# A list scheduler counts on more time between a transfer's wire time and its use, from the rolling pairs on

## Chip, core and metric

The kernel runs on one core of a Trainium2 chip. The metric is the device time of one execution in microseconds. Of the kernel before, three timed runs are shown, and one more execution that was recorded by the profiler.

## What is computed

Two blocks follow each other. The first is a retention attention without softmax, over 8 batches, 8 heads, 576 positions and a head dimension of 64, in float32. The second is a feed-forward block over the 4608 tokens, with a learned slope for negative values:

```python
scores = scale * np.matmul(q, k.transpose(0, 1, 3, 2))
Dmat = np.where(rel >= 0, gamma[:, None, None] ** rel[None, :, :], 0.0)
ret = scores * Dmat[None, :, :, :]
attn_out = np.matmul(ret, v)
# x: (B*S, H*D) = (4608, 512)
h = x @ w_in                                        # 512 x 2048
g = np.maximum(h, 0.0) + alpha * np.minimum(h, 0.0)
out = g @ w_out                                     # 2048 x 512
```

`rel` is the distance in positions between query and key, and each head has its own `gamma`. The two weight matrices arrive as 64-bit floats; the kernel reads them as pairs of 32-bit words and makes 32-bit floats of them on the chip.

## The kernel before

**Tiling.** The tokens are cut into 18 blocks of 256 (`kb`), the hidden dimension of 2048 into 8 units of 256 (`u`). A float32 operand of a large matmul is split into pieces of a shorter float format (a high part, a low part, and a difference), and three products of pieces replace one float32 product. Such a product is a matmul of 128 rows by 512 columns, L1187 and L1221 for the first layer and L1339 (in `second`) for the second layer.

**Stages.** A prologue computes the attention of the first two batches in wide pieces (`part_...`), converts the first 16 weight pieces, and runs eight cells in plain float32. Then come the *rolling pairs*: the other 24 head pairs of the attention, one after another, woven into the feed-forward work on the token blocks that are already finished, for the first half of the hidden units. The last stage runs the second half of the units for all blocks, two blocks side by side (`unit_two`), and needs no attention work any more.

**A head pair** is the function `joint`. Its keys and queries are loaded in eight pieces (`load_kq`, tiles `kx` and `qx`), its keys once more in another layout (`kn`), its values into `vn`. POOL scales `qx` (L832), DVE transposes both (L838), ACT scales `kn` (L843). TensorE then computes scores and sums over chunks of 64 positions (L919 and L922). DVE masks the scores into the tile `at` (L940); ACT and DVE accumulate the sums into `su` (L952 to L963). Two copies by DMA put the transposed queries beside the scores (`at<-qT`) and the sums beside the values (`vn<-su`). When they have landed, TensorE multiplies out the values (L860), and ACT copies these from the PSUM bank into the token block `x` (L879). `kx`, `qx`, `kn`, `kT`, `qT`, `at` and `su` have one buffer each, `vn` two.

**Weights.** Sixteen more pieces of the weights are converted between the pairs (`convert`): load into `op`, ACT (L729, L731), DVE (L739, L741, L750), POOL (L753), and a store from `wa` to the DRAM tile `wk`. They are read back after the pairs.

**What sets the order.** No order is written out. The kernel first records every operation as an `Op`, with its engine, a cost in microseconds, the operations that it depends on, and for a transfer a wire time `late` (bytes over a rate; 265 KB per us for most). `dues` then runs the list backward from the end and gives each operation a due time. `plan` runs it forward: on each engine, of the operations that can begin first, the one with the earliest due time is taken. Both ask `wait(d, op)` how long after `d` the operation `op` may begin: a constant if `d` is a transfer, nothing on the same engine, 0.2 us after TensorE, and 0.1 us otherwise. Twelve rounds of the two, and then 243 random shifts of the due times, keep the plan whose modelled total is the least. The operations are issued in that plan's order, on each engine's own queue; on the chip, semaphores make an instruction wait for what it needs, and planned times play no part.

Every transfer but one is issued on SP's queue, by the helper `dma` (L208). An instruction that waits there holds up all transfers behind it. TensorE's queue is in order too.

Of the kernel before, what the change touches and what calls it, by code (L numbers as in the profile page):

```python
# [21 lines left out]
def kernel(  # L22
# [24 lines left out]
    NKB = NTOK // TB  # L47
    NS = NU // 2
    NRING = 5

# [28 lines left out]
    def piece(x):  # L81
        return x.bitcast(PIECE)
# [35 lines left out]
    for i in range(NBIT - 1):  # L118
# [8 lines left out]
                            op=ALU.mult)  # L127
# [21 lines left out]

    ops = []

    class Op:
        def __init__(self, eng, cost, fn, deps, banks, late, lock, hold, size):
            self.eng, self.cost, self.fn, self.deps = eng, cost, fn, deps
            self.banks, self.late, self.lock, self.hold = banks, late, lock, hold
            self.size, self.n = size, len(ops)

    class Slot:  # L160
        def __init__(self, name, make, bank=False):
# [16 lines left out]
    def do(eng, cost, fn, r=(), w=(), late=0.0, lock=False, kind=None, hold=0.0, size=0):  # L178
        deps, gens = set(), []
        for keys, writes in ((r, False), (w, True)):  # L180
            for g, *sub in keys:
                wr, rd = g.keys.setdefault(tuple(sub), ([], []))
                deps.update(wr)
                if writes:
                    deps.update(rd)
                deps.update(g.before)
                if g not in gens:
                    gens.append(g)
        op = Op(eng, cost, fn, None, [g.slot for g in gens if g.slot and g.slot.bank], late, lock, hold,
                size)  # L190
        for g, *sub in w:
            g.keys[tuple(sub)] = ([op], [])
        for g, *sub in r:
            g.keys[tuple(sub)][1].append(op)
        for g in gens:
            assert not g.slot or g.slot.gen is g
            g.ops.append(op)
        op.deps = [d for d in deps if d is not op]
        op.gens, op.kind = gens, kind or eng
        ops.append(op)  # L200
        return op
# [22 lines left out]
    LAT = {"PE": 0.2}  # L224
# [1 line left out]
    users = []  # L226

    def wait(d, op):
        return 2.0 if d.late else 0.0 if d.eng == op.eng else LAT.get(d.eng, 0.1)

    def dues(after):
        users[:] = [[] for _ in ops]
# [11 lines left out]
        for _ in ops:  # L244
            pick = None
            for e, queue in ready.items():
                if queue:
                    t0 = min(max(free[e], can[op.n]) for op in queue)
                    op = max((op for op in queue if max(free[e], can[op.n]) <= t0 + 0.02),
                             key=lambda op: after[op.n])  # L250
                    t = max(free[e], can[op.n])
                    if pick is None or t < pick[0]:
                        pick = t, op
            t, op = pick
            ready[op.eng].remove(op)
            free[op.eng] = t + op.cost
            due[op.n] = -(t + op.cost)
            for d in op.deps:
                left[d.n] -= 1
                can[d.n] = max(can[d.n], t + op.cost + wait(d, op) + d.late)  # L260
                if not left[d.n]:
                    ready[d.eng].append(d)
# [88 lines left out]
    def slot(pool, tag, shape, dtype=FP32, bank=False):  # L351
        return Slot(tag, lambda: pool.tile(shape, dtype, tag=tag, name=f"{tag}_{next(serial)}"),
                    bank)
# [8 lines left out]
    def lx_all(which):  # L362
        if which not in lx_tiles:
            lx_tiles[which] = lpool.tile([P, 6 * NCC, TB], FP32, tag="lx", name=f"lx_{which}")
        return lx_tiles[which]

    def lx_slots(which):
        return [Slot(f"lx{n}", lambda n=n: lx_all(which)[:, 3 * NCC * n:3 * NCC * (n + 1)])
                for n in range(2)]
    lxs = lx_slots("w")  # L370
    xs = [slot(ring, f"x{n}", [P, NCC, TB]) for n in range(NRING)]
    os_ = [slot(ring, f"o{n}", [P, DM]) for n in range(2)]
# [180 lines left out]
    def chunk_home(x, j):  # L553
        kb, o = divmod(x // 3 * NJ + j, TB // C)
        if kb not in xb:
            xb[kb] = Gen(xs[kb % NRING])
        return xb[kb], o
# [240 lines left out]
    def load_kq(n):  # L798
        b, c = pairs[n]
        kx, qx = Gen(kxs), Gen(qxs)  # L800
        loaded[n] = [kx, qx, None, vnm[n % 2]]
        for g, src in ((qx, q), (kx, k)):
            for a in range(4):
                f0 = (a % 2) * 32
                dma(lambda g=g, a=a: g.get().rearrange("p (n r) -> p n r", r=32)[
                        32 * a:32 * a + 32],
                    lambda src=src, a=a, f0=f0: src[b, 2 * c + a // 2].rearrange(
                        "(n t) d -> t n d", t=32)[:, :, f0:f0 + 32], S * P, (), [(g, a)],
                    rate=RATE_128)

    def load_kn(n):
        b, c = pairs[n]
        kn = loaded[n][2] = Gen(kns)
        for h2 in range(2):
            dma(lambda h2=h2: kn.get()[half(1 - h2)],
                lambda h2=h2: k[b, 2 * c + h2].rearrange("(j t) d -> t j d", t=C), S * D * 4, (),
                [(kn, h2)], rate=RATE_256)
# [8 lines left out]
    def operands(n):  # L826
        c = pairs[n][1]
        kx, qx, kn, vn = loaded[n]

        def f():  # L830
            qh = qx.get().rearrange("p (j x r) -> p j x r", x=2, r=32)
            return nc.gpsimd.tensor_tensor(  # L832
                out=qh, in0=qh, in1=tabx[:, None, c, :, None].to_broadcast([P, NJ, 2, 32]),
                op=ALU.mult)
        do("POOL", 1.15, f, [(cst, "t")], [(qx, a) for a in range(4)], lock=True)
        kT, qT = turned[n] = Gen(kTs), Gen(qTs)
        for to, g in ((kT, kx), (qT, qx)):
            do("DVE", 0.77, lambda to=to, g=g: nc.vector.transpose(to.get(), g.get()),  # L838
               [(g, a) for a in range(4)], [(to, 0)])

        def f():
            t = kn.get().rearrange("p j d -> p (j d)")
            nc.scalar.activation(t, t, ACTF.Copy, scale=tabk[:, c:c + 1])  # L843
        do("ACT", 0.78, f, [(cst, "t")], [(kn, 0), (kn, 1)])
# [23 lines left out]
    def keep_x(n, pv, j1):  # L868
# [3 lines left out]
        while j < NJ:  # L872
            kb, o = divmod(b * NJ + j, w)
            if kb not in xb:
                xb[kb] = Gen(xs[kb % NRING])
            m, i = min(w - o, NJ - j), int(j >= j1)
# [114 lines left out]
    def fetch_x(vis):  # L991
        kb = vis["kb"]
        if kb in xb:
            x = xb.pop(kb)
            dma(lambda: x_kept[kb], lambda: x.get().rearrange("p c t -> p (c t)"), P * 4096,
                [(x, *s) for s in x.keys], [(xkm[kb], 0)], hold=HOLD_X)
        else:
            x = Gen(xs[taken[0] % 2])
            taken[0] += 1
            dma(lambda: x.get().rearrange("p c t -> p (c t)"), lambda: x_kept[kb], P * 4096,  # L1000
                [(xkm[kb], 0)], [(x, 0)])
        vis["from"] = x
# [137 lines left out]
    def row_x(side, l):  # L1140
        return (3 * side + (l if side else 2 - l)) * NCC

    def split_roll(vis):
        fetch_x(vis)
        x, side = vis["from"], vis["kb"] % 2
        g = vis["x"] = Gen(lxs[side])
        keys = [(x, *s) for s in x.keys]

        def view(l, n):
            r = row_x(side, l) + 2 * n  # L1150
            return lambda: lx_all("x")[:, r:r + 2]

        def raw(n):
            return x.get()[:, 2 * n:2 * n + 2]
        for n in range(2):
            h, l, d = (view(l, n) for l in range(3))
            do("ACT", 0.64, lambda n=n, h=h: nc.scalar.mul(piece(h()), raw(n), BELOW * 2.0 ** -12),
               keys, [(g, 0, n)])
            do("DVE", 0.70, lambda n=n, h=h, l=l: nc.vector.scalar_tensor_tensor(  # L1159
                out=piece(l()), in0=h(), scalar=-2.0 ** 12, in1=raw(n), op0=ALU.mult, op1=ALU.add),  # L1160
                keys + [(g, 0, n)], [(g, 1, n)], lock=True)
            do("POOL", 1.29, lambda h=h, l=l, d=d: nc.gpsimd.tensor_tensor(  # L1162
                out=piece(d()), in0=h(), in1=l(), op=ALU.subtract),
                [(g, 0, n), (g, 1, n)], [(g, 2, n)], lock=True)
# [222 lines left out]
    def joint_(x):  # L1387
        joint(x)
        done.add(x)
        if x + 1 < len(pairs):  # L1390
            load_kn(x + 1)
            operands(x + 1)
        if x + 2 < len(pairs):
            load_kq(x + 2)
# [219 lines left out]
        Gen(x).before = was_in  # L1614
    for _ in range(EARLY):
        joint_(next(todo))
    split_roll(visits[2])
    last = singles - 1
    t = 8
# [126 lines left out]
```

## Time and profile before

| what | us |
| --- | --- |
| median of three runs | 925.6 |
| lowest and highest run | 923.88 and 931.11 |
| the profiled execution's own time | 921.56 |
| its span | 919.6 |
| TensorE busy (share of the span) | 909.4 (99%) |
| weight loads | 737.3 (80%) |
| DVE, ACT, POOL busy | 547.3, 505.2, 519.5 |
| share of the 16 DMA engines' span, main queue | 52.4% |

The span is the time from the first instruction to the last; the execution's own time has 1.96 us around it. TensorE's busy time is made of modelled ends of pipelined matmuls, so that a short hole can be hidden in it; weight loads (PEld) lie beside the matmuls and have durations of their own. The profile also tells, for a transfer, the time from its issue to its landing, and for each wait which engine or transfer ended it. The first of the 24 scores blocks runs at about 90 us, the last values block at 439 us; from there to the end no pair is in the way.

### The profile page before, as it was taken

The numbers are of one execution on the slowest core, as the hardware profiler recorded it, in microseconds if no ns is written. First come the engines' busy times: TensorE is split into PE (matmuls) and PEld (weight loads), VectorE is DVE, ScalarE is ACT, GpSimd is POOL, SyncE is SP. The second block draws the span as 40 slices with busy tenths as digits, with TensorE's granted clock in tenths as the row PEclk, the third lists the DMA queues.
The fourth block names the chain that finished last, engine by engine and source line by source line (L and its number), as shares of the span: only waits on it lengthen the run. The fifth ranks groups of instructions, "written<-read, shape, count | busy, mean of one in ns | idle before, by whom it ended". The sixth has DMA issues, their size and how long they took to land. (4 is left out here: it accounts for less than half of the span.)

```text
span 919.6 us, 19101 instructions
## 1 busy us (share of the span) xinstructions
PE 909.4 (99%) x7289; PEld 737.3 (80%) x7289; DVE 547.3 (60%) x1003; ACT 505.2 (55%) x1010; POOL 519.5 (56%) x461
## 2 busy tenths in 40 slices
PE   8999999999999999999999999999999999999998
PEld 7776688888888887878888788888888888888886
DVE  6878767567676757576757776444444444444343
ACT  4575555646665655666746655536464636364441
POOL 4766746555565656666453247465656656574624
PEclk9999999999999999999999999999999999999999
DMA  9994787886898968885345331212221222211112
GB/s 214 262 230 80 181 194 173 192 185 143 178 186 204 207 137 215 168 183 159 127 143 190 116 116 56 92 57 81 81 79 43 95 95 68 84 54 47 47 46 68
DMA packets 235947, 121.32 MB, mean 132 GB/s; under 512 B 203456, under 2 KB 203728, under 8 KB 235856
## 3 DMA queue, kind: packets, MB, share of 16 engines
q1 hardware_dynamic: 235712, 119.98, 52.4%
q8 instruction: 57, 0.93, 0.5%
q14 instruction: 34, 0.28, 0.1%
q10 hardware_dynamic: 144, 0.13, 0.0%
HBM read 74.19 MB, written 32.51 MB: 116 GB/s over the span
## 5 line engine op out<-in xcount | busy, mean ns | idle before, releaser
L1339 PE MATMUL pso<-w,g 128*128 128x512 f32 x1392 | 339.2, 392 | 0.4
L1339 PEld LDWEIGHTS pso<-w,g 128*128 128x128 f32 x1392 | 259.0, 188 | 57.7 <-POOL g L1266 2.7
L1263 POOL TENSOR_TENSOR g<-ga_all,g 128x512 fp32r<-128x512 f32 x76 | 98.0, 1291 | 121.9 <-ACT g L1259 93.9
L1266 POOL TENSOR_TENSOR g<-g 128x512 fp32r<-128x512 f32 x114 | 147.3, 1293 | 16.6 <-DVE w L1065 4.4
L1187 PE MATMUL psh<-lx_x,w 128*128 128x512 f32 (+1 forms) x360 | 87.4, 381 | 0.0
L1187 PE MATMUL psa<-lx_x,w 128*128 128x512 f32 (+1 forms) x360 | 84.5, 375 | 0.0
L1187 PEld LDWEIGHTS psh<-lx_x,w 128*128 128x128 f32 x360 | 63.9, 188 | 13.9 <-issue 0.5
L1187 PEld LDWEIGHTS psa<-lx_x,w 128*128 128x128 f32 x360 | 64.7, 188 | 12.6 <-ACT kn L843 0.3
L1259 ACT ACTIVATE g<-ga_all 128x512 fp32r<-128x512 f32 x76 | 47.7, 631 | 41.6 <-PE pso L1339 21.8
L1162 POOL TENSOR_TENSOR lx_x<-lx_x 128x512 fp32r<-128x512 f32 x28 | 35.8, 1288 | 39.8 <-DVE lx_x L1159 36.9
L1263 POOL TENSOR_TENSOR g<-vn,g 128x512 fp32r<-128x512 f32 x25 | 32.4, 1294 | 41.9 <-ACT g L1259 37.4
L1255 POOL TENSOR_TENSOR g<-g 128x512 fp32r<-128x512 f32 x22 | 28.4, 1293 | 46.7 <-DVE g L1252 29.6
L940 DVE SCALAR_TENSOR_TENSOR at<-psa,pf,mask 64x512 f32<-64x512 f32 x48 | 36.0, 749 | 31.5 <-PE psa L919 27.1
L1339 PE MATMUL pso<-lx_x,g 128*128 128x512 f32 x216 | 53.3, 390 | 0.1
L1357 DVE TENSOR_TENSOR op<-pso,op 128x512 f32<-128x512 f32 x35 | 24.0, 685 | 41.4 <-PE pso L1339 41.3
L1261 ACT ACTIVATE g<-ga_all 128x512 fp32r<-128x512 f32 x76 | 47.2, 621 | 1.2 <-PE pso L1339 1.0
L1339 PEld LDWEIGHTS pso<-lx_x,g 128*128 128x128 f32 x216 | 40.4, 188 | 9.0 <-DVE o L1362 0.7
L753 POOL TENSOR_TENSOR wa<-wa,op 128x512 int32<-128x512 int32 x16 | 20.9, 1309 | 36.1 <-DVE wa L750 18.6
L860 PEld LDWEIGHTS psh<-at,vn 128*64 128x64 f32 x864 | 27.8, 137 | 10.0 <-issue 6.0
L1201 ACT COPY ga_all<-psh 128x512 f32<-128x512 f32 (+1 forms) x30 | 16.7, 557 | 33.0 <-PE psh L1187 26.1
L1221 PE MATMUL psh<-w,w 128*128 128x512 f32 x144 | 34.6, 389 | 0.0
L1221 PE MATMUL psa<-w,w 128*128 128x512 f32 x144 | 34.6, 389 | 0.0
(329 smaller groups left out, 1882.3 us busy)
## 6 DMA issues: line engine op xcount, KB each, us to landing
xk<-x SPq DMA_DIRECT2D x18, 512.0 KB, 4.0
ok<-o SPq DMA_DIRECT2D x36, 256.0 KB, 3.0
op<-ok SPq DMA_DIRECT2D x18, 512.0 KB, 3.9
out_dram<-o SPq DMA_DIRECT2D x35, 256.0 KB, 2.2
x<-xk SPq DMA_DIRECT2D x16, 512.0 KB, 4.8
qx<-in_q_dram SPq DMA_DIRECT2D x96, 72.0 KB, 3.2
kx<-in_k_dram SPq DMA_DIRECT2D x96, 72.0 KB, 3.4
kn<-in_k_dram SPq DMA_DIRECT2D x48, 144.0 KB, 3.6
```

Source lines behind the costliest of these rows:

```text
L860: nc.tensor.matmul(pv[i].get()[half(h2), (j - js[0]) * C:(j - js[0] + 1) * C], vns[n % 2][:, h2, j], mt.get()[:, h2, j], start=True, stop= ...
L940: nc.vector.scalar_tensor_tensor(out=mt.get()[half(1 - h2), h2, j], in0=fro[x], scalar=pf[x, 1, h:h + 1], in1=mask[x, None, :].to_broadcas ...
L1162: do("POOL", 1.29, lambda h=h, l=l, d=d: nc.gpsimd.tensor_tensor(out=piece(d()), in0=h(), in1=l(), op=ALU.subtract), [(g, 0, n), (g, 1, n) ...
L1187: nc.tensor.matmul(out_of(p), w[:, c0:c0 + P], xp(l, cc), start=(l != 1 and cc == 0), stop=(l > 0 and cc == NCC - 1))
L1221: nc.tensor.matmul(p.get(), w[:, c0:c0 + P], piece(words_of(g)[:, o:o + DM]), start=(l != 1 and cc == 0), stop=(l > 0 and cc == NCC - 1))
L1255: do("POOL", 1.29, lambda: nc.gpsimd.tensor_tensor(out=piece(to.get()[:, 2]), in0=to.get()[:, 0], in1=to.get()[:, 1], op=ALU.subtract), [( ...
L1259: do("ACT", 0.64, lambda: nc.scalar.mul(piece(to.get()[:, 2]), whole(), BELOW), both, [(to, 2)])
L1261: do("ACT", 0.64, lambda: nc.scalar.mul(piece(to.get()[:, 0]), whole(), BELOW * 2.0 ** -12), both, [(to, 0)])
L1263: do("POOL", 1.29, lambda: nc.gpsimd.tensor_tensor(out=piece(to.get()[:, 1]), in0=whole(), in1=to.get()[:, 2], op=ALU.subtract), both + [( ...
L1266: do("POOL", 1.29, lambda: nc.gpsimd.tensor_tensor(out=piece(to.get()[:, 2]), in0=to.get()[:, 0], in1=to.get()[:, 1], op=ALU.subtract), [( ...
L1339: nc.tensor.matmul(a[2 * m + b].get(), piece(g.get()[:, l, f, m * P:(m + 1) * P]), w_piece(u, 2 + f, l), start=(cell["first"] and f == 0 a ...
L1357: do("DVE", 0.69, lambda: nc.vector.tensor_tensor(out=t(), in0=p1.get(), in1=t(), op=ALU.subtract), [(p1, 0)], [tk])
```

## The change

From the moment at which the first rolling pair's work has been recorded, every new operation carries 3.5 instead of 2.0 as the time that the scheduler counts between the end of its wire time and its first use. Operations recorded earlier keep 2.0. The value is used in both directions, by `dues` and by `plan`. No operation, dependency, buffer or cost is altered otherwise.

```diff
     NRING = 5
+    LAND = 2.0, 3.5
...
-    ops = []
+    ops, land = [], [LAND[0]]
...
             self.banks, self.late, self.lock, self.hold = banks, late, lock, hold
-            self.size, self.n = size, len(ops)
+            self.size, self.n, self.land = size, len(ops), land[0]
...
     def wait(d, op):
-        return 2.0 if d.late else 0.0 if d.eng == op.eng else LAT.get(d.eng, 0.1)
+        return d.land if d.late else 0.0 if d.eng == op.eng else LAT.get(d.eng, 0.1)
...
     for _ in range(EARLY):
         joint_(next(todo))
+    land[0] = LAND[1]
     split_roll(visits[2])
```

The order in which each engine's instructions stand differs after the change almost from the first instruction, since due times are counted from the end.

## Prediction

> **What bounds the kernel now.** I read the page's first two parts for the busiest engine, then busy time in 20 us stretches, then the waits, then the time that transfers take to land.
>
> The first two parts of the page:
>
> ```profile
> span 919.6 us, 19101 instructions
> ...
> PE 909.4 (99%) x7289; PEld 737.3 (80%) x7289; DVE 547.3 (60%) x1003; ACT 505.2 (55%) x1010; POOL 519.5 (56%) x461
> ```
>
> TensorE is busy for 909.4 of 919.6 us, so 10.2 us are visibly idle. Where these lie is seen in stretches of 20 us (columns: span, busy us and count of PE, PEld, DVE, ACT, POOL, then the granted clock, DMA share and GB/s):
>
> ```profile
> 0.00:20.00 20.00, 15.94 (x345) 13.39 (x346) 11.58 (x51) 7.45 (x12) 8.91 (x22) 1.00 1.02 202
> ...
> 160.00:180.00 20.00, 19.90 (x185) 15.95 (x185) 13.07 (x24) 11.01 (x23) 8.71 (x7) 1.00 0.81 187
> ...
> 300.00:320.00 20.00, 20.00 (x274) 16.54 (x273) 15.23 (x29) 13.39 (x29) 12.80 (x11) 1.00 1.00 218
> ...
> 400.00:420.00 20.00, 19.51 (x177) 15.46 (x175) 14.40 (x28) 13.46 (x26) 11.27 (x9) 1.00 1.08 241
> ...
> 500.00:520.00 20.00, 19.86 (x87) 15.86 (x86) 14.55 (x23) 11.35 (x21) 6.32 (x5) 1.00 0.43 133
> ...
> 740.00:760.00 20.00, 20.00 (x90) 16.57 (x89) 8.35 (x12) 8.23 (x15) 9.09 (x9) 1.00 0.33 106
> ...
> 900.00:919.60 19.60, 15.55 (x69) 11.86 (x67) 7.99 (x13) 2.42 (x4) 6.92 (x6) 0.98 0.25 80
> ```
>
> The first stretch is idle for 4.06 us and the last for 4.05. Between 20 and 100 us it is 1.33 more (0.42 and 0.91), and from 100 to 900 us, where the change acts, 0.73 (0.10, 0.49 and 0.14). The modelled ends of matmuls can hide a hole, so I also compare weight loads with a full stretch: 740 to 760 has 16.57 us of them for 90 matmuls at 222 ns each. A stretch short of that by x has lost about x/16.57 of 20 us: 500 to 520 lost 0.86, the four stretches with 16.30 to 16.32 about 0.3 each. Among the rolling pairs, full stretches show 16.5; 160 to 180 lost 0.67 us and 400 to 420 lost 1.26, the four with 16.05 to 16.33 together 1.4. **All holes from 100 to 900 us come to 5.4 us**, 0.6% of the time.
>
> No wait of TensorE is charged to a transfer in the list of waits; the largest wait for one on any engine belongs to ScalarE, which is idle for it rather than late:
>
> ```profile
> ACT kn L843 <- DMA kn<-in_k_dram: 16.4, 13, 2.8
> ```
>
> The Trainium skill, "Perfetto Trace Analysis", "Identifying the Most-Contended Engine", holds matmul busy time to be a bad measure of headroom and weight-load share a better one. By that, 80% would leave 182 us. The stretch at 740 us speaks against reading it so: it runs one matmul per 222 ns without a hole and shows 83%.
>
> **The change, part by part.** It removes and adds no instruction: both programs hold the same 5,343 matmul instructions and 619 transfers on SP's queue. It alters an assumption, so I first ask which value is right. Landing times of the issues (KB each, median us from issue to landing):
>
> ```profile
> kx<-in_k_dram SPq DMA_DIRECT2D x96, 72.0 KB, 3.4
> kn<-in_k_dram SPq DMA_DIRECT2D x48, 144.0 KB, 3.6
> ...
> at<-qT SPq DMA_DIRECT2D x48, 144.0 KB, 3.3
> vn<-su SPq DMA_DIRECT2D x48, 128.0 KB, 3.4
> ...
> wk<-wa SPq DMA_DIRECT2D x16, 256.0 KB, 3.6
> ```
>
> For at<-qT the scheduler counts 0.56 us of issue, 147,456 B at 265 kB per us = 0.56 of wire, then the constant: 3.12 us with 2.0, 4.62 with 3.5. Measured: 3.3. In the same way vn<-su gives 3.05 or 4.55 against 3.4, kn 3.28 or 4.78 against 3.6, wk 3.55 or 5.05 against 3.6. **The old constant is short by 0.05 to 0.35 us, the new one long by 1.15 to 1.45.** The change thus adds cover of over 1 us to each transfer, which the median transfer doesn't need.
>
> The Trainium skill, "DMA: Bandwidth & Descriptors", "Anatomy of one DMA", speaks against the change: a fixed cost of about 2.0 us plus bytes over 436 GB/s (fitted for another issue path). An estimate from it for at<-qT is 2.34 us; the row gives 3.3 less 0.59 of issue, 2.7. By either, 3.5 is cover and no correction.
>
> *Matmul order.* Between the scores and sums of a pair (L919, L922) and its values (L860) stand 10.9 us of other PE work in the median before and 12.1 after (512-column matmuls at 227 ns start to start in that order). In 11 of 23 steps the next pair's scores now stand wholly ahead of the values, where it was 3. TensorE has other work in that place, so the moves cost nothing by themselves; what hides them is the 10 to 12 us of 512-column matmuls per pair. They change between small and large matmuls 61 times where it was 59; a neighbouring 335 ns start to start against 227 prices a change at 0.11 us: **+0.2 us**. If the cover were gone, a pair would wait for its transfer's remainder, 3.4 us at most.
>
> *Bank reuse.* The attention's values and the first matmul form share banks. The shortest distances in PE work from the last use of psh0 to its next owner were 0.7, 1.4, 1.8, 1.8, 1.8 us, and are 0.7, 0.8, 1.4, 1.4, 1.4. The eviction that must fit in between (L879) takes 0.34 us in the median and often waits its turn on ScalarE. From nothing to 1 us for each of three places: 0 to +3; I take the middle, **+1.5 us**, since the 0.7 of before opened no visible hole.
>
> *Weight conversions.* Sixteen round trips (op load, L729 to L753, wk store) form a chain on two single buffers. Counted back from their use, each is now 3 us longer (two landings), so the chain starts earlier: the first load stands after the at transfer of the ninth pair counted, before after the thirteenth; the first store after the twelfth instead of the sixteenth. When the last pair's at transfer is issued, 11 stores are queued ahead of it instead of 8, and 80.5 MB instead of 78.1. These 2.4 MB fall into 200 to 420 us, where the DMA share averages 0.84 (0.71 to 1.08) and the rate 182 GB/s, 40 MB in all: 6% more, a share of 0.89. The three conversions bring 3 x 1.55 us to DVE and 3 x 1.31 to POOL in 220 us, where these are 69% and 57% busy. Nothing on TensorE waits for a conversion before 500 us. At SP a wk store waits for L753, and what stands behind it is the next pair's loads; SP's issues take 0.3 to 0.65 us each. Cost: between nothing, and what the fullest stretch lost (1.26 us at a share of 1.08) in one more stretch. I take **+0.5**.
>
> *Holes that may close.* 0.67 + 1.26 us in two stretches of the pairs, whose order changes; none is charged to a transfer, so between nothing and 1.9: **-1.0**. The 0.86 at 500 us lies at the end of the conversion chain, which starts earlier but ends in the same place: 0 to -0.9, **-0.4**.
>
> *Start and tail.* Transfers before the pairs keep 2.0, yet their order moves too, since all due times are counted from the end: k, k, q, q where it was k, q, k, q. The first 100 us have 5.4 us of idle time; I put this between -2 and +3 and take **0**. The last 556 matmul instructions and the last 54 of DVE and of POOL stand as before, so the tail keeps its 4 us.
>
> **Sum:** 0.2 + 1.5 + 0.5 - 1.0 - 0.4 = +0.8 us on the profiled execution's own 921.6 us. The runs shown have a median of 925.6, 4.0 above it; there the same gives 926.4, and I say **926 us**.
>
> **Rivals.**
> *Cover pays.* The runs shown go from 923.9 to 931.1, the profiled one is at 921.6. If late landings make that difference, over 1 us of extra cover takes most of it: about 921.5 (-0.4%). For: these spreads are unexplained. Against: no wait of TensorE for a transfer in the profile. It can't reach 1% (9.3 us): all holes of its part are 5.4, and with 5.4 of the start barely 10.8.
> *The rewritten order does nothing:* semaphores, not planned times, release instructions, and the same work flows within +-1 us: 925.6. This is the forecast in all but its decimals.
> *Transfers crowd.* Slower: the earlier conversions push the pair stage to a full DMA. Price 1.26 us per stretch; if all eleven from 200 to 420 lost it, 13.9 us, 939.5. It is slower by 1% from eight such stretches on, a mean share of about 1. For: 300 to 320 and 400 to 420 are there already. Against: 6% more is 0.89.
> *Order too tight elsewhere.* Three bank places as above recur in more pairs: 1 us in each of ten pairs, 935.6.
>
> **How the numbers follow.** One per cent, 9.3 us, is about what a measurement here can tell from no change. Forecast and do-nothing 0.62, cover pays 0.12 (0.08 of it within 1%, 0.04 more with a lucky start), crowding 0.13, tight order 0.13. Of the last two, 0.02 stays within 1%. So faster 0.04, within 1% 0.72, slower 0.24. The range goes from 919 (cover pays, and 2 us of the start) to 936 (ten tight pairs).
>
> **What would show it.** Right: PE still 99%, weight loads near 16.5 per stretch from 100 to 900 us, at and vn landing in 3.3 to 3.5 us, longer gaps between a landing and its use. Wrong: stretches among the pairs below 16 us of weight loads, a DMA share above 1 in several of them, landings over 4.5 us, or waits of PE at L860 for a transfer or at psh for ScalarE.

## Result, and the profile after

| what | before | after |
| --- | --- | --- |
| median of 11 runs each (us) | 923.88 | 919.44 |
| lowest and highest run | 921.6 and 931.11 | 917.86 and 920.88 |
| ratio of the means, with its 95% interval | | 0.9943 (0.992 to 0.9965) |
| profiled execution (us) | 921.56 | 919.19 |

The changed kernel is 0.6% faster by the means: 4.4 us lie between the medians, and only 2.4 us between the two profiled executions, because the one profiled before the change was as quick as that kernel's quickest run.

The first two parts of the page of the kernel after (span, then busy us of each engine):

```profile
span 917.4 us, 19097 instructions
...
PE 906.9 (99%) x7289; PEld 737.8 (80%) x7289; DVE 548.0 (60%) x1003; ACT 503.9 (55%) x1010; POOL 520.2 (57%) x461
```

The kernel after in the same stretches of 20 us (span, busy us and count of PE, PEld, DVE, ACT, POOL, then granted clock, DMA share, GB/s):

```profile
0.00:20.00 20.00, 15.49 (x347) 13.43 (x348) 10.69 (x51) 7.15 (x12) 8.96 (x22) 1.00 0.99 213
...
160.00:180.00 20.00, 20.00 (x182) 16.57 (x181) 13.89 (x24) 11.63 (x23) 9.10 (x8) 1.00 0.88 182
...
220.00:240.00 20.00, 19.85 (x253) 15.73 (x253) 14.52 (x28) 11.62 (x25) 13.32 (x11) 1.00 0.76 169
...
300.00:320.00 20.00, 20.00 (x275) 16.52 (x274) 12.98 (x24) 12.96 (x28) 13.31 (x12) 1.00 0.91 216
...
400.00:420.00 20.00, 20.00 (x202) 16.42 (x202) 16.07 (x30) 12.83 (x25) 11.37 (x9) 1.00 0.98 213
...
500.00:520.00 20.00, 20.00 (x90) 16.58 (x89) 14.33 (x24) 10.78 (x21) 5.19 (x4) 1.00 0.29 85
...
900.00:917.40 17.40, 13.39 (x60) 10.30 (x59) 7.99 (x13) 1.47 (x3) 4.92 (x4) 1.00 0.29 90
```

The three holes that the prediction named are gone: weight loads rose from 15.95 to 16.57 us at 160, from 15.46 to 16.42 at 400, and from 15.86 to 16.58 at 500. One stretch got worse: 220 to 240 us shows 15.73, where it was 16.05. From 100 to 900 us the weight loads rose by 2.4 us in all. The tail is idle for 4.0 us as before, the first stretch for 4.5 instead of 4.1, and no stretch among the pairs shows a DMA share over 1 any more.

ScalarE's largest wait for a transfer, in the waits of the kernel after (us in total, times, longest us):

```profile
ACT kn L844 <- DMA kn<-in_k_dram: 7.2, 5, 3.2
```

It was 16.4 us in 13 times. The transfers did not get faster. These issues of the kernel after (KB each, median us from issue to landing) land as before, within 0.2 us; `x<-xk` lands later, 5.6 us after its issue instead of 4.8:

```profile
kx<-in_k_dram SPq DMA_DIRECT2D x96, 72.0 KB, 3.3
kn<-in_k_dram SPq DMA_DIRECT2D x48, 144.0 KB, 3.4
at<-qT SPq DMA_DIRECT2D x48, 144.0 KB, 3.4
vn<-su SPq DMA_DIRECT2D x48, 128.0 KB, 3.5
...
wk<-wa SPq DMA_DIRECT2D x16, 256.0 KB, 3.6
```

What changed is the order of the work around them. The first place to look is the hole at 400 us of the kernel before. Its timeline there (start us, busy us, then the instruction, and in brackets how long its engine had been idle before it, and what ended that):

```profile
402.60 0.65 ACT L731 ACTIVATE op<-op 128x512 int32<-128x512 uint32 x1 [1.01 <-DMA op<-in_moe_w_out_dram]
...
404.14 0.43 DVE L739 TENSOR_SCALAR wa<-wa 128x512 f32<-128x512 f32 x1 [1.77 <-ACT wa L729]
...
406.39 1.37 PEld L860 LDWEIGHTS psh<-at,vn 128*64 128x64 f32 x36 [0.35 <-DVE ga_all L1202]
...
408.63 0.27 PE L922 MATMUL psa<-vn,kn 64*64 64x64 f32 x1 [0.36 <-DVE ga_all L1207]
```

ScalarE stands at the head of its queue for a weight piece that has not landed. DVE then stands for ScalarE's result (L729), although its queue also holds, behind the next steps of the conversion, L1202 and L1207, the evictions that free PSUM banks. These come late, and TensorE waits for them twice. The list of waits names DVE as what TensorE waited for; the transfer is two queues further back. A second profiled execution of the kernel before (922.73 us) and a third (926.31 us) have holes at the same place, and larger ones; in the third, by the same steps:

```profile
404.52 0.78 ACT L845 ACTIVATE kn<-kn,tabk 128x576 f32<-128x576 f32 x1 [1.64 <-DMA kn<-in_k_dram]
...
407.71 0.68 ACT L733 ACTIVATE op<-op 128x512 int32<-128x512 uint32 x1 [1.93 <-DMA op<-in_moe_w_out_dram]
...
409.15 0.43 DVE L741 TENSOR_SCALAR wa<-wa 128x512 f32<-128x512 f32 x1 [2.58 <-ACT wa L731]
...
411.02 0.33 PE L862 MATMUL psh<-at,vn 128*64 128x64 f32 x2 [0.42 <-DMA vn<-su]
```

Here TensorE also waits for a transfer itself, `vn<-su`, as in the second execution (0.7 and 0.6 us in all): a late landing with no wait of ScalarE or DVE in between. DVE had finished the copy's source at 403.36 us; SP, still issuing other transfers, came to it at 405.13.

ScalarE, DVE and POOL wait 4.7, 8.7 and 8.3 us for `op` from 100 to 440 us in the three executions before, and 1.4 us after. From 340 to 440 us the weight loads come to 80.9, 79.4 and 79.5 us before, and to 82.0 after. The hole at 160 us is another matter: the second and third execution don't have it (16.43 and 16.54 us of weight loads), so it came and went in one and the same order, and its closing isn't shown to be the change's work. The hole at 500 us is in all three; what causes it wasn't followed.

The time between a load and its use can be read off directly. In the kernel before, the timeline shows 17 issues of loads of weight pieces into `op` between 250 and 500 us; from issue to ScalarE's first use they have 4.75 us in the median, and 3.97 at the least. In the kernel after, the 16 such issues from 200 us on have 5.88 in the median and 5.21 at the least. The load behind the hole, in the timeline of the kernel before, with its use 4.72 us later (402.60, above):

```profile
397.88 0.57 SPq L208 DMA_DIRECT2D op<-in_moe_w_out_dram  x1
```

One at a like place of the kernel after, with 5.48 us to its use, where ScalarE no longer waits:

```profile
403.16 0.44 SPq L209 DMA_DIRECT2D op<-in_moe_w_out_dram  x1
...
408.64 0.68 ACT L732 ACTIVATE op<-op 128x512 int32<-128x512 uint32 x1
```

### The profile page after: what moved, and what is told of

It reads as the page before. It is cut to its first block, busy times and chain, and to the rows that moved or that the text cites. A ratio compares the mean times of both kernels' runs of the same rounds, so it can differ in the third digit from the quotient of the medians.

```text
span 917.4 us, 19097 instructions
## 1 busy us (share of the span) xinstructions
PE 906.9 (99%) x7289; PEld 737.8 (80%) x7289; DVE 548.0 (60%) x1003; ACT 503.9 (55%) x1010; POOL 520.2 (57%) x461
## 5 line engine op out<-in xcount | busy, mean ns | idle before, releaser
L1264 POOL TENSOR_TENSOR g<-ga_all,g 128x512 fp32r<-128x512 f32 x76 | 97.9, 1291 | 130.4 <-ACT g L1260 105.0
L1202 ACT COPY ga_all<-psh 128x512 f32<-128x512 f32 (+1 forms) x30 | 16.7, 558 | 39.1 <-PE psh L1188 37.4
```

The costliest lines, as they stand in the source:

```text
L1264: do("POOL", 1.29, lambda: nc.gpsimd.tensor_tensor(out=piece(to.get()[:, 1]), in0=whole(), in1=to.get()[:, 2], op=ALU.subtract), both + [( ...
```

## Experiments

The theory after the result: **the constant gives cover against late landings, which reach TensorE through ScalarE's and DVE's queues.** The rival: **the new constant only draws another plan**, and plans differ by some microseconds by luck. Ratios are of means, against the kernel before, run on the same chip in the same comparison. "From the pairs on" is the span less the start of the first matmul of the rolling first layer (L1187), in the profiled execution.

### The cover put in and taken out by hand

`e1_old_later` takes the plan of the kernel before, and places every operation of ScalarE, DVE and POOL that directly uses a transfer, from the rolling pairs on, 1.5 us later in the order; `e2_new_sooner` takes the plan of the kernel after and places them 1.5 us sooner.

```diff
+    SHIFT = 1.5                       # e2: LAND = 2.0, 3.5 and SHIFT = -1.5
+    key = list(best[2])
+    for op in ops:
+        if op.n >= n_roll and op.eng in ("ACT", "DVE", "POOL") and any(d.late for d in op.deps):
+            key[op.n] += SHIFT
...
-    for op in best[1]:
+    for op in out_of_order:           # by key, as dependencies allow
```

> The plan of the kernel before (constant 2.0, the same due times and matmul order up to what follows), but every ACT, DVE and POOL operation of the pairs and after that uses a transfer directly is set 1.5 us later in the plan and so stands behind a few more operations of its own engine. No transfer is issued earlier and the plan isn't drawn anew. Theory 'cover' (an ACT, DVE or POOL operation that waits for a late transfer at the head of its in-order queue holds up evictions behind it, and TensorE through them): the idle time that a transfer ends on these engines from 100 us on, 26.8 us in the profile before, falls below 15, and the time goes to 919 to 921 us, a ratio of 0.994 to 0.998. Rival 'redraw' (the new constant only made the random search land on another plan that happens to be better): the plan is the old one, so 0.998 to 1.006, since the moved operations are also late for their own users.

> The plan of the changed kernel, with the same operations set 1.5 us earlier: matmuls and transfers keep their order, only ACT, DVE and POOL queues differ. Theory 'cover': the waits for transfers on ACT, DVE and POOL from 100 us on rise from 14 us to over 25, and the gain is given back: ratio to the kernel before 0.998 to 1.003. Rival 'redraw': the plan is the new one, so it stays at 0.993 to 0.996.

Measured: e1 966.32 us, ratio 1.0444 (1.0395 to 1.0494); e2 937.27 us, 1.0143 (1.0105 to 1.018). Both theories missed both runs. In e1, the waits of TensorE from 100 to 900 us (us in total, times, longest) hold these rows:

```profile
PE pso L1341 <- DVE o L1364: 5.5, 6, 1.9
PE pso L1341 <- POOL g L1268: 5.3, 9, 1.0
PE psh L1189 <- ACT x L881: 4.5, 5, 1.7
...
PE psh L862 <- DMA vn<-su: 0.3, 1, 0.3
```

The users of transfers include evictions of PSUM banks, whose target buffer an output store must have left. Placed later, they keep TensorE without banks: it is visibly idle for 17.85 us from 100 to 440 us and for 10.48 from there to 900, where the kernel before has 0.59 and 0.14. Of a landing almost nothing is charged. In e2 the waits of ScalarE, DVE and POOL that a transfer ended, summed from 100 to 440 us, are 14.0 us, as in the kernel after (13.6), and not more, as cover would have it; TensorE is idle there for 7.96 us in many short waits for results of those engines. Both edits move far more than the suspected cause, and **decide nothing between the theories**; they do show that the place of these operations, by 1.5 us, is worth tens of microseconds when the rest of the plan doesn't follow.

### Other draws of both plans

The plan is the best of 243 random shifts. Another seed gives another plan under the same constants, and so prices luck.

```diff
+    LAND = 2.0, 2.0                   # e3, e7, e15;  2.0, 3.5 in e4, e8, e16
...
-    rng = np.random.RandomState(1)
+    rng = np.random.RandomState(2)    # e3, e4;  3 in e7, e8;  4 in e15, e16
```

> The constant stays 2.0; only the seed of the random search over due times is another. It measures what a new draw alone is worth. Theory 'cover': 921 to 928 us, ratio 0.998 to 1.004, with over 20 us of waits for transfers on ACT, DVE and POOL from 100 us on. Rival 'redraw': draws differ by 4 us and more, and this one may be anywhere from 918 to 930.

> The constant 3.5 with another seed. Theory 'cover': again 918 to 921 us, ratio 0.992 to 0.997. Rival 'redraw': anywhere from 918 to 930, and as likely above 922 as below.

> The constant 2.0 with a third seed. After seeds 1 (923.4 us) and 2 (919.9 us): 'redraw' says that the plan of the kernel before is an unlucky draw, so about 919 to 922 us here; 'cover' says that 2.0 leaves plans fragile, so 922 us or more, or runs that differ by over 5 us.

> The constant 3.5 with a third seed. After seeds 1 (919.4 us) and 2 (918.8 us): 'cover' says 918 to 920 us with runs that differ by 3 us at most; 'redraw' says 918 to 924 us, the same span as for 2.0.

> Constant 2.0, fourth seed; the three before gave 923.9, 919.9 and 923.4 us. 'Cover': above 920.5 us. 'Only the draw': as likely below 920 as above.

> Constant 3.5, fourth seed; the three before gave 919.4, 918.8 and 917.5 us. 'Cover': below 920 us. 'Only the draw': as likely above 920 as below.

`e5_before_again` and `e6_before_third` are the kernel before with the re-sorting lines and a shift of 0, for two more profiled executions of the same order.

> The kernel before once more, for a second profile. Its runs go from 920.9 to 931.1 us, those of the changed kernel from 917.9 to 920.9. Theory 'one fragile place': an execution near 925 us has lost the 4 us over the first profile in one or two places of the pair stage, where a late transfer holds up an in-order queue, and these are the places around 408 and 412 us or others like them. Rival 'spread everywhere': the loss is in many stretches, or in the first 100 us, which no constant of the pairs reaches.

> The same for a third profile: with the two others it shows which holes of TensorE recur in every execution of this plan and which come and go. 'Fragile place': the same instructions lose time each time, by different amounts, together 2 to 8 us. 'Spread everywhere': no hole recurs.

They took 922.73 and 926.31 us, so the profiled 921.56 was a quick one. All draws:

| seed | constant 2.0: median, ratio | first L1187, from the pairs on | constant 3.5: median, ratio | first, from the pairs on |
| --- | --- | --- | --- | --- |
| 1 | 923.88 | 104.3, 815.3 (103.6, 817.2; 106.7, 817.9) | 919.44, 0.9943 | 105.0, 812.4 |
| 2 | 919.86, 0.9953 (0.9932 to 0.9973) | 103.3, 813.5 | 918.75, 0.9941 (0.9922 to 0.996) | 104.1, 812.8 |
| 3 | 923.35, 0.9994 (0.9975 to 1.0012) | 109.2, 812.2 | 917.49, 0.994 (0.9919 to 0.9961) | 104.8, 810.7 |
| 4 | 924.78, 1.0004 (0.9986 to 1.0023) | 108.1, 814.6 | 917.04, 0.991 (0.9878 to 0.9942) | 104.4, 811.6 |

In brackets are the second and third profiled execution. The four draws with 3.5 are all below the four with 2.0, by 4.8 us in the mean of the medians (918.2 against 923.0); had the constant no influence, that order would come by chance once in 70. So it is hardly luck alone. The waits say so too: ScalarE, DVE and POOL together wait for transfers for 20.0 to 32.2 us from 100 to 440 us in the six profiled executions with 2.0, and for 3.4 to 13.6 us in the four with 3.5. So every draw with 3.5 waits less for landings. Yet luck is large: the second draw with 2.0 comes within 0.5 us of the kernel after. And about half of the 4.8 us isn't the cover's own: with the three executions of seed 1 averaged, the start takes 106.4 us in the mean with 2.0 and 104.6 with 3.5 (1.8 us), a stage whose transfers keep 2.0 in both and whose order is only drawn anew, and in which stops come and go in a single profile (last section); from the pairs on it is 814.3 against 811.9 (2.4 us), and the ranges overlap (812.2 with 2.0, 812.8 with 3.5). For seed 1, the pair of kernels of this study, the difference lies wholly from the pairs on: 816.8 against 812.4 us.

`e16_new_seed4` is the best version of the study, 917.04 us: its highest run, 917.74, is under the lowest of the kernel after, 917.86.

### ScalarE's three users alone

To follow the chain shown above, only L843 (`kn`) and the two conversion steps L729 and L731 are moved: 1.5 us later in the plan of before (e9), 1.5 us sooner in that of after (e10). All other queues keep their order.

```diff
-           [(a, "a")])
+           [(a, "a")]).soft = True       # likewise L731 and L843
...
+        if op.n >= n_roll and op.soft:
+            key[op.n] += SHIFT            # 1.5 in e9, -1.5 in e10
```

> The plan of the kernel before with one thing moved: on ScalarE the scaling of kn (L843) and the two activations on a freshly loaded weight piece (L729, L731) stand 1.5 us later in the plan, so behind a few more ScalarE operations. TensorE, DVE, POOL and SP keep their order to the instruction, and nothing is drawn anew. Theory 'head of the queue' (a late kn or op transfer blocks ScalarE, then DVE through L739, then evictions and TensorE): the holes at 360, 393 and 405 to 413 us shrink, waits of ACT for kn and op from 100 to 440 us fall from 18 to 21 us below 8, time 920 to 922.5 us, ratio 0.996 to 0.9985. Rival 'only the draw counts': no gain, 0.9985 to 1.003, as the operations are then late for DVE and for the next scores.

> The plan of the changed kernel with the same ScalarE operations 1.5 us sooner; all other queues as they are. 'Head of the queue': the waits of ACT for kn and op rise from 8 us to over 20 and part of the gain is lost: ratio to the kernel before 0.996 to 1.000. 'Only the draw counts': 0.993 to 0.9955, no change against the changed kernel.

Measured: e9 932.48 us, 1.0096 (1.0056 to 1.0137), the wrong way; e10 919.42 us, 0.9949 (0.9929 to 0.997), no loss. The timeline of e9 around a hole of 2.4 us:

```profile
386.36 0.44 SPq L211 DMA_DIRECT2D op<-in_moe_w_out_dram  x1
...
392.17 0.66 ACT L734 ACTIVATE op<-op 128x512 int32<-128x512 uint32 x1 [5.16 <-DMA op<-in_moe_w_out_dram]
...
394.43 0.43 DVE L742 TENSOR_SCALAR wa<-wa 128x512 f32<-128x512 f32 x1 [8.26 <-ACT wa L732]
...
395.97 1.43 PE L1342 MATMUL pso<-w,g 128*128 128x512 f32 x5 [2.38 <-DVE o L1365]
```

`op` has one buffer, so the load can begin only when the conversion before it has left. In the kernel before, that set its time: POOL's L753 ended at 380.15 + 1.31 = 381.46 and SP issued the load at 381.49. In e9 it didn't. POOL's step ended at 384.85, later by the 3.4 us by which this whole execution is behind there, but SP was still issuing `kx` and sent the load only at 386.36:

```profile
383.12 3.13 SPq L211 DMA_DIRECT2D kx<-in_k_dram  x4
```

So the load went out 1.5 us later than the shift explains, and took 5.8 us to its use instead of 5.0. ScalarE waits again (`op` 6.0 us in all where it was 4.2; only `kn` fell, from 13.7 to 2.3, all from 100 to 440 us), and DVE, whose order wasn't moved, waits 8.26 us. Giving the user a later place didn't remove the wait, as the load came later by more. Why SP's issues and the landing took longer here is not shown, nor how much of the 8.4 us lost (924.03 us beside it) is this. In e10 ScalarE's waits for `kn` rise from 6.4 to 11.4 us, and no time is lost: as the prediction said, those are idle and not late.

### The constant on a part of the transfers

`e11_conv_only` gives 3.5 to the loads and stores of the sixteen conversions alone, `e12_pairs_only` to the transfers of the pairs alone.

```diff
     def convert(raw, wa, to, c=None):
+        land[0] = LAND[to is None]        # e11; back to LAND[0] at its end
...
     def joint_(x):
+        land[0] = LAND[len(rolling)]      # e12; back to LAND[0] at its end
```

> A new plan in which only the transfers of the sixteen weight conversions among the pairs (op loads, wk stores) carry 3.5; all others 2.0. If the conversions are the fragile part: waits of ACT for op gone, those for kn stay above 8 us, 918 to 921 us. If the pairs' own transfers are: as the draws with 2.0, 920 to 923.5 us.

> A new plan in which only the transfers of the pairs (kx, qx, kn, vn, at, and the sums) carry 3.5; conversions, token blocks and outputs 2.0. If the pairs' transfers are the fragile part: waits of ACT for kn below 5 us, those for op still 4 to 6 us, 918 to 920 us. If the conversions are: 920 to 923.5 us.

Measured: e11 927.21 us, 1.0031 (1.0012 to 1.005); e12 922.48 us, 0.9978 (0.9956 to 1.0001). Weight loads are full at 400 us in both (16.62 and 16.56 us). In e11 no wait for `op` is listed any more from 100 to 440 us, and the time still doesn't fall: it has a new hole at 115 us, after which the granted clock falls (0.96 from 100 to 120 us). The hole, in its waits of TensorE from 100 to 440 us:

```profile
PE psh L863 <- DVE ga_all L1205: 2.6, 1, 2.6
```

e12 keeps 15.93 us of weight loads at 500 us and falls to 15.75 at 360. Either half closes the hole at 400 us, and each draw has its own holes elsewhere. Neither half is the whole.

### The loads made short, in the same order

If the late `op` loads make the hole, loads that can't be late must close it with the plan of before untouched. Here the sixteen conversions fetch a quarter of the bytes and read it four times over, and one of ScalarE's two steps (L731) reads a constant tile in place of the load, so the second half of the hidden units is computed with wrong weights; `e13_old_op_quarter` has the order of before, `e14_new_op_quarter` that of after, as a control.

```diff
-                lambda src=src: src, P * DM * 8 // len(srcs), (), [(g, "r", off, i)])
+                lambda src=src, n=n: src[:, 0:n] if part else src, P * DM * 8 // len(srcs), (),
+                [(g, "r", off, i)])
...
+            x = flat().rearrange("p (f two) -> p f two", two=2)[:, 0:P, i]
+            return x[:, None, :].to_broadcast([P, 4, P])
```

> The plan of the kernel before, every queue in its order, but the op loads of the sixteen conversions among the pairs fetch a quarter of their bytes, so they land earlier; ACT and DVE read that quarter four times over, and L731 reads a constant tile (the second half of the hidden units is thus computed with wrong weights). Nothing else is left out. If late op loads cause the holes of the kernel before at 360, 393 and 405 to 413 us: these go, ACT's waits for op from 4 to 6.5 us to below 2, and the time to 919.5 to 921.5 us, ratio 0.9955 to 0.998. If the order itself is bad there (evictions behind long DVE work): the holes stay, 922 to 924.5 us, ratio 0.9985 to 1.001.

> The control: the same cut of the op loads in the plan of the changed kernel, where ACT waits 1.4 us in all for op. Both readings: within 1 us of the changed kernel, 918.4 to 920.0 us. If it gains 2 us or more, the cut helps in another way (fewer bytes on the queues), and the run with the old plan says less.

Measured: e13 920.9 us, 0.9963 (0.9943 to 0.9982), 3.7 us less in the median than the kernel before beside it (924.58; 1.7 to 5.3 by the interval of the means); e14 918.98, 0.9939 (0.9912 to 0.9965), 0.5 us from the kernel after. The stretch with the hole, in e13:

```profile
400.00:420.00 20.00, 19.97 (x242) 16.28 (x237) 15.58 (x33) 13.11 (x29) 14.08 (x12) 1.00 0.80 174
```

and ScalarE's waits for transfers from 100 to 440 us, all of them:

```profile
ACT kn L859 <- DMA kn<-in_k_dram: 15.3, 12, 3.2
ACT o L1151 <- DMA ok<-o: 0.7, 1, 0.7
```

The waits for `op` are gone and those for `kn` are as large as ever (13.7 us before): so it was the `op` loads that cost, and not the `kn` loads, which have the largest row in the list. From 340 to 440 us the weight loads come to 81.7 us, where the three executions of the same order had 79.4 to 80.9; the hole at 500 us stays (16.09). By the medians most of the 4.4 us come back without any change of plan; by the profiled executions, from the pairs on, about half (814.5 us, against 816.8 in the mean before and 812.4 after). Left open is how much of it was the loads' own lateness, and how much the room that shorter loads leave to others (the DMA share from 100 to 440 us falls from 0.81 to 0.75): no wait of TensorE for `vn<-su` is listed either.

### Other sizes

```diff
+    LAND = 2.0, 2.75                  # e17;  2.0, 5.0 in e18
```

> The constant 2.75 from the rolling pairs on, seed 1. The median landings ask for 2.1 to 2.4 (2.0 and the 0.05 to 0.35 us by which it is short). If covering the median is enough, 917 to 920 us as with 3.5; if the late ones in the tail matter, between the two groups, 920 to 922.5 us.

> The constant 5.0, seed 1. If more cover still helps: 916 to 918 us. If 3.5 covers what comes, 917 to 920 us. If the pairs' chains no longer fit between the matmuls in the plan, over 921 us, with waits for transfers on ACT, DVE and POOL from 100 to 440 us still below 15 us.

Measured: 2.75 gives 926.71 us, 1.0028 (1.001 to 1.0045); 5.0 gives 922.97, 0.9985 (0.9962 to 1.0008). From the pairs on they take 818.2 and 816.3 us. If cover were the whole story, 5.0 would be no worse than 3.5, and 2.75 no worse than 2.0. Their waits for transfers are small (16.1 us with 2.75 and 13.3 with 5.0, counted as above), but TensorE is visibly idle for 1.06 and 2.55 us from 100 to 440 us, by rows that name DVE, ACT and POOL; in the kernel after it is 0.15. Cover alone doesn't make a plan good. One draw each can't tell a size that doesn't work from a bad draw: draws with one constant differ by 2 to 5 us. **What stays open** is therefore how much of the 2.4 us from the pairs on belongs to 3.5 as such.

## Why the prediction was right or wrong

**Right: no large change.** The time fell by 0.6%, within the 1% that was given 0.72, and within the range. But the forecast was 926 us, slightly slower, and the interval of the ratio is only 0.2% to either side: the 1% that I took for what a measurement can tell was too coarse.

**Right in part: the holes close.** The two terms for holes, -1.0 and -0.4, were bounded by 1.9 and 0.9 us of lost weight loads. By the same measure (x/16.57 of 20 us) the three stretches gained 0.75, 1.16 and 0.87 us, 2.8 in all: the upper bounds, where I had taken about half. But the 0.75 at 160 us isn't in the other two executions of the kernel before, so that part of the gain came by luck as far as the runs show, and the stretch at 220 us lost 0.4 us.

**Wrong: the cover was priced at nothing.** The step is "No wait of TensorE is charged to a transfer in the list of waits", with its conclusion that the change adds cover "which the median transfer doesn't need". Both halves are true, and the conclusion isn't. An in-order queue is stopped by the late landing and not by the median one: the load issued at 381.49 us was used at 386.48, after ScalarE had waited 3.20 us for it, so it took nearly 5.0 us, where the median of such loads is 4.4. And the list of waits names only the last releaser. Followed two queues back, TensorE's wait for DVE is a wait for `op`; e13 took those waits away and got 3.7 us back (1.7 to 5.3). One profile also was too few: in the two others TensorE is charged with a wait for `vn<-su`. The row that I showed, `kn` with 16.4 us, was rightly called idle (e10 and e13 confirm it): the largest wait for a transfer was harmless, and one of 4.2 us did the harm, because DVE's evictions stood behind it.

The Trainium skill says in "Perfetto Trace Analysis", "Optimization Strategy", to find the gaps on the engine of interest and what blocks them, by semaphore and by the instruction that updates it. The timeline at 402 to 409 us agrees, and shows that the step has to be repeated on each engine that is found: the first answer was DVE L1207, the third the load. The rule I had weighed, "DMA: Bandwidth & Descriptors", "Anatomy of one DMA", gives one fixed cost of about 2.0 us, for another issue path. A fixed cost tells nothing of late landings, and those are what the cover is for: the two loads that ScalarE stood longest for took 4.7 and 5.0 us from issue to use.

**Wrong: bank reuse, +1.5.** No trace of it: TensorE's waits from 100 to 440 us don't grow, and its busy time there rose from 339.41 to 339.85 us. Shorter distances in PE work stayed wide enough for an eviction of 0.34 us. The term is 1.5 of the 5.2 us between the +0.8 of the sum and the -4.4 that was measured; the holes are another 1.4 of them, and the conversions 0.5.

**Weight conversions, +0.5.** The chain did start earlier (first load issued at 208.07 us instead of 254.63), but no stretch got crowded: the DMA share from 200 to 420 us rose from 0.84 to 0.86, not to 0.89, and at 400 us it fell from 1.08 to 0.98. (Two readings there were off: the share went from 0.52 to 1.08, and DVE and POOL were busy for 68% and 60%.) The earlier chain has 5.9 us from issue to use, and ScalarE stands only 1.4 us in all for its loads. That an earlier conversion chain alone is a gain isn't shown: e11, which gives 3.5 to nothing else, is no faster.

**Matmul order +0.2, start 0, tail 0.** The profiled start went from 104.3 to 105.0 us to the first L1187 (103.6 and 106.7 in the other executions of before), so 0.7 us were lost there, within the -2 to +3; the tail kept its 4 us, as said. The order's 0.2 is too small to be seen.

**One profile was taken for the kernel.** I put the sum on the profiled 921.56 us and moved it up by 4.0 to the median, as if the difference were the same after the change. The two other executions lose 1.9 and 2.6 us more from the pairs on than that one (817.2 and 817.9 against 815.3 us), most of it from 340 to 440 us, where the waits for `op` are: the 4.0 us were in part the very lateness that the change covers. The median of three runs was high as well: of eleven it is 923.88 and not 925.6. The spread also shrank, from 9.5 to 3.0 us between lowest and highest. That was the rival *Cover pays*, "if late landings make that difference", with its 921.5 us, or -0.4%; it got a chance of 0.12 and came nearest, with the mechanism of the holes as it had it. *Transfers crowd* and the tight order didn't happen; *the rewritten order does nothing* is excluded by the interval, though the draws show that a rewritten order alone can be worth 4 us (919.86 against 923.42 beside it). The signs that I named for being right all came: 99%, stretches near 16.5 us (but for the one at 220 us), landings of 3.4 and 3.5 us. They fitted *Cover pays* just as well, and so couldn't tell the two apart.

## What to carry to other kernels

A wait list ends at the nearest engine: when the bounding engine waits for an evicting engine, follow that engine's queue to its head, and then the next, until a transfer or a full buffer is found; the size of a wait for a transfer says little, what stands behind it in the queue says more. A scheduler's constant is judged over several draws of the plan and several profiles of each, since one draw is worth as much as the constant: here plans under 2.0 spread over 5 us, and the study's best is 3.5 with another seed, 917.04 us. Moving a user later by hand, in a plan that is otherwise kept, made the kernel slower here (e9) and doesn't replace a plan made anew. A hole that one profile shows may be gone in the next of the same order, as the one at 160 us was.

## What the runs showed of the hardware that was not expected

The start stage has a hole of its own that comes and goes in the same program order. At about 30 us, in the midst of identical 64x64 matmuls, TensorE stops with no releaser in the profile. One such stop, in the waits of TensorE of e9 (us in total, times, longest):

```profile
PE psh L601 <- issue: 3.0, 1, 3.0
```

It stands in 8 of the 20 profiled executions, with 0.3 to 3.0 us; among five executions whose TensorE order is that of the kernel before (the first three, e9, e13) it is none, none, 0.7, 3.0 and 2.0. Of the five stops of 2.0 us and more, four come with a fall of the granted clock. e9, in stretches of 4 us (columns as above, the clock is the third from the end):

```profile
32.00:36.00 4.00, 3.07 (x29) 1.92 (x30) 2.59 (x4) 2.16 (x4) 3.44 (x4) 0.64 1.12 277
36.00:40.00 4.00, 4.00 (x17) 1.91 (x17) 2.08 (x3) 2.42 (x5) 1.11 (x2) 0.93 1.06 213
```

the same in e13, with a stop of 2.0 us:

```profile
32.00:36.00 4.00, 4.00 (x30) 1.97 (x30) 3.16 (x5) 2.42 (x4) 3.44 (x4) 0.50 1.19 260
36.00:40.00 4.00, 4.00 (x12) 2.10 (x12) 1.44 (x3) 2.22 (x4) 1.10 (x2) 0.50 1.02 216
```

and in the profiled execution of the kernel before, without a stop:

```profile
32.00:36.00 4.00, 4.00 (x19) 2.20 (x18) 3.68 (x6) 2.66 (x5) 3.45 (x4) 1.00 1.04 240
```

The first L1187 comes at 107.8 us in e9 and 109.7 in e13, where it was at 104.3: with stop and slower clock the start is 3.5 and 5.4 us longer, in a part that the edits don't touch, and e13's profiled execution (926.2 us, the slowest of its ten runs) shows how far one profile can mislead. The Trainium skill, "TensorE: Matmul & The Clock Gate", "Part 1: The HAM clock gate", has the clock halve after an idle window of about 3.4 us that runs freely. The 0.50 agrees, and so do the times for which the packed traces have it: 3.41 us in e9, 6.83 in `e1_old_later` and 10.24 in e13, once, twice and three times the same window. That e2 keeps 1.00 after a stop of 2.8 us fits a whole window too. But in e13 the clock is down 1.5 us after the stop began, and in e7 after a wait of 1.7 us for DVE; a whole idle window would not give that.

What makes TensorE stop wasn't tried, but the packed traces point to its instructions. All eight stops stand before the same matmul, the 604th that is recorded, though the plans differ. The fourth 16 KB piece of the queue that the profile calls "instruction" (q8) had ended 1.4 to 2.0 us before each of these stops was over: in e9 it ran from 29.96 to 31.40 us, and TensorE went on at 32.93. In the kernel before, without a stop, it had ended at 28.22. That a late piece of instructions holds TensorE up is thus likely, and not proved.
